# A lag of three chunks beside the attention, a staging tile that outlives it, and new due times: sparse attention followed by two feed-forward layers on one Trainium2 core

## The chip, the cores and the metric

The kernel runs on one core of one Trainium2 chip, as one program. The metric is the device time of the program in microseconds. Timed runs are separate executions; the profile is one further execution, taken by the hardware profiler. The engines are TensorE (PE, with its weight loads as PEld), VectorE (DVE), ScalarE (ACT), GpSimd (POOL) and SyncE (SP), which only issues DMAs.

## The reference

```python
# q, k, v: (4, 8, 576, 64), tau: a number
scores = scale * np.matmul(q, k.transpose(0, 1, 3, 2))          # scale = 1/8
thresh = np.max(scores, axis=-1, keepdims=True) - tau
scores = np.where(scores >= thresh, scores, -1000000000.0)
attn = softmax(scores)                                          # in words here
x = (attn @ v) laid out as (2304 tokens, 512)
h = x @ w1_in                                                   # (2304, 2048)
g = np.where(h > 0.0, h, np.exp(np.minimum(h, 0.0)) - 1.0)
x = g @ w1_out                                                  # (2304, 512)
h = x @ w2_in
out = np.maximum(0.01 * h, h) @ w2_out
```

## The kernel before, in words

**Attention.** The 32 heads are taken in pairs, and the 576 rows of queries of a batch in two groups, of 4 and of 5 units of 64 rows (`GROUPS`). So there are 4 batches x 2 groups x 4 pairs = 32 groups. Two units at a time go through this line: TensorE makes the scores s into two PSUM banks (L475), VectorE scales them and takes the maximum (L479) and the threshold (L485), ScalarE cuts (L490) and exponentiates (L493), VectorE inverts the sum (L496), GpSimd multiplies by it (L498). The result e then has to be turned. For the first four groups TensorE turns it (L513) and ScalarE or VectorE copies it to p (`copies`, by `kc`). For the other 28 VectorE turns it in blocks of 32 (L518) and 16 DMAs per group bring the blocks to their places (L568): `NG` of the 16 are issued by GpSimd, the others by SyncE. Then TensorE makes v, the product of p and the values (L582), and a copy puts it into x.

**Feed-forward.** The hidden width of 2048 is cut into 16 chunks of 128. A chunk of h needs 12 products (4 chunks of x times 3 products of rounded parts, since each fp32 operand is split into a high part, xh, gh, wih, woh, and a low part, xl, gl, wil, wol); a chunk's share of y needs 12 too. Between them stand the steps of g: exponential (L639, ScalarE), minus one (L641 on VectorE or L643 on GpSimd, by `km`), maximum with h (L647, VectorE), rounding to gh (L313 ScalarE, L311 GpSimd, by `kg`) and the subtraction that gives gl (L307 VectorE, L308 GpSimd). While the attention runs, the first 7 blocks of 256 tokens go through the first 8 chunks of layer 0 ("beside the attention"); the very first of them uses plain fp32 products (L621, L674). After it, the remaining 512 tokens go through the same 8 chunks, then all 2304 tokens through the other 8 and then through layer 1, in blocks of 512.

**Lag and buffers.** In `block`, the products of y for chunk j are made after those of h for chunk j + `LAG`; `moe_rings` gives gh and gl `LAG + 1` buffers. h has two halves of one PSUM bank. The sums of y of a block are copied to the tile ysa (`evac_a`), and that is written to DRAM (L731, yp).

**Order.** No engine's order is written by hand. Every step becomes an `Op` with dependencies, a due time `vt` and a list of engines with costs. `Order.run` goes through time and on each free engine starts the ready step that is due first; the instructions are emitted in that order, and on the chip the engines wait for each other by semaphores. All due times come from the table `KN`: `boff`, `bdt`, `yoff` and `mo` place the blocks beside the attention, the time per chunk, the products of y and the steps of g; `o1` to `o6` the steps of the attention; `wv0`, `wv1`, `wp0` the weights; `vl` the loads of the values. On TensorE, `stay` lets a step of the same kind as the last one (plain fp32, or rounded) go first if it is due no more than that many ns after the first in line.

**The end of the attention.** `end_a` is a step of the planner that closes the pools of the attention and opens those of the rest over the same memory. It waits for every step that has been listed up to it.

Of the kernel before, what the change touches and what calls it, by code (L numbers as in the profile page):

```python
# [10 lines left out]
F32 = mybir.dt.float32  # L11
F32R = mybir.dt.float32r
# [9 lines left out]
NP = NH // 2  # L22
# [7 lines left out]
NU = S // 64  # L30
GROUPS = [(b, u0, u1) for b in range(B) for u0, u1 in ((0, 4), (4, NU))]
UM = 5
WT = 32 * UM
BESIDE = 7
GP = 1
PT = ()
NG = 5
POOLI = 520
SPI = 720
PM = ()  # L40
# [4 lines left out]
SX = 640  # L45
LAG = 2
TAUX = 100.0
LN9 = -20.72326583694641
# [3 lines left out]
KN = dict(  # L52
    pad=18, stay=1957.74, late=1.3, margin=0, look=0.00236881, warm=2, tu=2525.65, lead=19496.6, wv0=975.379,
    wv1=-2861.01, early=3673.33, boff=26347.2, bdt=5788.03, yoff=6965.78, coff=5895.83, wb=140.292, w2a=-207.297,
    b0=0, b1=0, b2=0, bd0=9322.68, vl=22862.5, tl=13509.4, wp0=137202, wp1=-2346.6, o1=-5700.07, o2=1859.51,
    o3=-792.8, o4=-3200.93, o5=4767.88, o6=-24.0285, mo=-2162.59, ka='P', kl='PA', kh='PA', ko='P', kt='D', kx='A',
    kxl='DP', km='DP', kg='A', kgl='DP', kgl1='D', kd='P', kc='AD', kn='P', kv='AD')

# [204 lines left out]
def attn_moe_kernel(ctx, tc, kqv, tau, w1i, w1o, w2i, w2o, yp, out):  # L263
# [19 lines left out]
    wa_r = ring(stg, 1, [128, 512], F32, "wa_")  # L283
    ysx = []
    ys_r = Ring(lambda: ysx[-1], 1)
# [77 lines left out]
    def moe_rings(pool, w):  # L363
        xr = [[ring(pool, 1, [128, w], F32R, f"x{z}{k}") for z in "hl"] for k in range(KC)]
        return xr, ring(pool, 2, [128, w], F32, "g"), *(ring(pool, LAG + 1, [128, w], F32R, n) for n in ("gh", "gl"))

# [12 lines left out]
    rings = {True: moe_rings(sbuf(aes, "ma"), TA)}  # L379
    ysx.append(ac.tile([128, KC, TA], F32, name="ysa"))  # L380
    taut = ac.tile([128, 1], F32, name="taut")
# [45 lines left out]
    def group(gi, p, vts, held=None):  # L427
# [23 lines left out]

        by_pe = gi < GP or p in PT
        which = len(p_r.gens) % 2
# [10 lines left out]
        def units(js, vt):  # L464
# [4 lines left out]
            def qk():  # L469
                for z, j in enumerate(js):  # L470
                    for h in range(2):
                        for i in range(2):
# [11 lines left out]
                             out=thr()[:, 0:m], in0=nm()[:, 0:m], scalar1=taup, scalar2=1.0, op0=ALU.add, op1=ALU.mult)),  # L484
                         D=(150, lambda: nc.vector.tensor_scalar(  # L485
                             out=thr()[:, 0:m], in0=nm()[:, 0:m], scalar1=taup, scalar2=None, op0=ALU.add))),
# [201 lines left out]

    ypdone = {}

    def block(layer, t0, fs, tb, deps, hps, yrings, evac, vt0, dt, reg=False):
        if reg and t0 < NATIVE * TA:
            xc = [(None, x[:, k, t0:t0 + tb], deps[k]) for k in range(KC)]
        else:
            xc = conv_x(t0, tb, deps, vt0 - dt + (KN["coff"] if reg else 0), reg)
        pend, lasty = [], None
        if isinstance(yrings, Ring):
            gen = yrings.new()
            ybank = [(gen, m % 2, m % 2 == 1) for m in range(KC)]

            def ysl(yg, m):
                return yg()[:, m // 2, m % 2 * TA:(m % 2 + 1) * TA]
        else:
            ybank = [(r.new(), 0, True) for r in yrings]

            def ysl(yg, m):
                return yg()[:, 0:tb]
        for n in range(len(fs) + LAG):
            if n < len(fs):
                pend.append(step_h(layer, fs[n], tb, xc, hps, vt0 + n * dt, reg))  # L710
            if n >= LAG:
                j = n - LAG
                lasty = step_y(layer, fs[j], j == 0, j == len(fs) - 1, tb, pend[j], ybank, ysl,
                               vt0 + n * dt + (KN["yoff"] if reg else 1))
        evac(t0, tb, ybank, ysl, lasty, xc, vt0 + len(fs) * dt)

    def evac_a(t0, tb, ybank, ysl, last, xc, vt):
        ys = ys_r.new()
        done = []
        if ybank[0][0] is ybank[1][0]:  # L720
            yg = ybank[0][0]
            for j in range(2):
                done.append(op(copy_of("AD", 2 * TA, lambda j=j: ys()[:, 2 * j:2 * j + 2, 0:TA],
                                       lambda j=j: yg()[:, j, :].rearrange("p (a b) -> p a b", a=2)),
                               [last[2 * j], last[2 * j + 1]], [yg, ys], vt))
# [33 lines left out]
    for b in range(B):  # L759
        mine = [gi for gi, g in enumerate(GROUPS) if g[0] == b]  # L760
        order += [(gi, p) for p in range(NE) for gi in mine] if b in PM else [(gi, p) for gi in mine for p in range(NE)]
    kept, ready = None, {}
    for gi, p in order:
        b, u0, u1 = GROUPS[gi]
# [5 lines left out]
        held = later  # L770
        if gi < GP or p in PT or u == NP * NU:
            held()
            held = None
# [14 lines left out]

    for i in range(BESIDE):
        need = next(n for t, n in ends if t >= (i + 1) * TA)  # L790
        block(0, i * TA, list(range(FH)), TA, x_deps(i * TA, TA), h_a, ya, evac_a,
              need * TU + KN["boff"] + (KN["b0"], KN["b1"], KN["b2"], 0)[min(i, 3)], KN["bd0"] if i == 0 else KN["bdt"],
              reg=True)
        if i == NATIVE - 1:
# [3 lines left out]

    end_a = op((HOST, 0, lambda: close_attn()), list(od.ops), [], 0)
    late_pool = []  # L800
# [14 lines left out]

    rest = [(t0, tb) for t0, tb in ((t, min(TB, NT - t)) for t in range(BESIDE * TA, NT, TB))]
    ysb = {}
# [75 lines left out]
```

## Time and profile before

| | us |
|---|---|
| three timed runs | 1047.26, 1040.55, 1043.79 |
| their median | 1043.79 |
| the profiled execution | 1044.41 |
| its span from first to last instruction | 1042.6 |
| mean granted clock of TensorE | 0.992 of full speed |

The 0.6 us by which the profiled execution lies above the median are less than the runs differ among themselves. The span leaves out 1.8 us around the program. In the rows below, times are in us from the start of the span unless marked ns, and L475 is line 475 of the kernel. Ends of matmuls are modelled, so rows of TensorE overlap; the distance of two starts is the better measure of what a product takes.

### The profile page before, as it was taken

How to read it: one execution, taken by the hardware profiler on the slowest of the kernel's cores; microseconds unless marked ns; L12 is line 12 of the kernel's file. 1: busy time of each engine (PE TensorE's matmuls, PEld its weight loads, DVE VectorE, ACT ScalarE, POOL GpSimd, SP SyncE). 2: the span in 40 equal slices, each digit the busy share in tenths (PEclk: the TensorE clock that was granted, in tenths of full speed). 3: DMA queues.
4: the chain of work that ended last, by engine and by line, in shares of the span. 5: the costliest groups of instructions: out<-in, count | busy, mean ns of one | idle time of the engine just before them, and what ended most of it. 6: DMA issues, size and time to landing. Idle time of an engine off the chain costs nothing.

```text
span 1042.6 us, 17014 instructions
## 1 busy us (share of the span) xinstructions
PE 1005.2 (96%) x6228; PEld 795.3 (76%) x6228; DVE 569.2 (55%) x1146; ACT 507.0 (49%) x1009; POOL 392.0 (38%) x542
## 2 busy tenths in 40 slices
PE   6869999999999998999999999999999999999998
PEld 3446676677676776888888889888888888888898
DVE  6888778787887856767786457442211311311121
ACT  6967767677777753555455235432222311322221
POOL 5678977567577752444443013440000000000000
PEclk8999999999999999999999999999999999999999
DMA  6676876766778653353443103320100100000010
GB/s 213 209 216 175 221 195 192 227 188 196 201 209 240 192 150 119 102 182 101 143 141 101 61 21 86 118 61 0 41 1 1 41 1 1 22 19 1 1 41 21
DMA packets 47554, 115.93 MB, mean 111 GB/s; under 512 B 9776, under 2 KB 14384, under 8 KB 47472
## 3 DMA queue, kind: packets, MB, share of 16 engines
q1 hardware_dynamic: 42960, 104.36, 33.4%
q0 software_dynamic: 4512, 10.50, 3.7%
q8 instruction: 49, 0.80, 0.3%
q14 instruction: 33, 0.27, 0.1%
HBM read 67.63 MB, written 9.44 MB: 74 GB/s over the span
## 4 chain that ended last, share of the span: by engine, by line
PE 90%; DVE 3%; DMA 2%; ACT 2%; issue 1%; POOL 0%; SPq 0%; ACTq 0%; DVEq 0%; POOLq 0%
PE y L678 37%; PE h L624 22%; PE hb L624 15%; PE v L582 7%; PE s L475 7%; PE y L674 1%; DMA p<-t 1%; PE h L621 1%; DVE w L346 1%; DMA taut<-in_tau_dram 1%; DVE ss L479 1%; DMA wraw<-in_w1i_dram 1%; PE y L513 0%; DVE xl L307 0%; ACT e L493 0%
## 5 line engine op out<-in xcount | busy, mean ns | idle before, releaser
L307 DVE TENSOR_TENSOR gl<-g,gh 128x512 fp32r<-128x512 f32 (+1 forms) x150 | 101.1, 675 | 284.4 <-ACT g L656 265.0
L678 PE MATMUL y<-gh,woh 128*128 128x512 f32 (+1 forms) x704 | 245.5, 349 | 2.1 <-ACT ysa L318 1.4
L678 PE MATMUL y<-gl,woh 128*128 128x512 f32 (+1 forms) x704 | 242.8, 345 | 0.0
L624 PE MATMUL h<-xh,wih 128*128 128x256 f32 (+1 forms) x448 | 153.1, 342 | 9.2 <-ACT g L639 5.1
L678 PEld LDWEIGHTS y<-gh,woh 128*128 128x128 f32 x704 | 132.5, 188 | 29.1 <-issue 8.8
L624 PE MATMUL h<-xl,wih 128*128 128x256 f32 (+1 forms) x448 | 148.6, 332 | 0.7 <-DVE xl L307 0.6
L678 PEld LDWEIGHTS y<-gl,woh 128*128 128x128 f32 x704 | 132.7, 188 | 16.1
L498 POOL TENSOR_SCALAR e<-e,su 128x576 f32<-128x576 f32 x144 | 113.9, 801 | 32.2 <-DVE su L496 30.9
L678 PE MATMUL y<-gh,w 128*128 128x256 f32 (+1 forms) x384 | 124.9, 325 | 0.0
L490 ACT ACTIVATE ss<-ss,thr 128x576 f32<-128x576 f32 x144 | 104.6, 767 | 34.5 <-DVE thr L485 34.4
L479 DVE TENSOR_SCALAR_CACHE_REDUCE ss<-s,scl 128x576 f32<-128x576 f32 x144 | 113.8, 798 | 10.9 <-PE s L475 10.7
L678 PE MATMUL y<-gh,wol 128*128 128x512 f32 (+1 forms) x320 | 117.7, 368 | 0.0
L518 DVE STREAM_TRANSPOSE t<-e 128x640 f32<-128x640 f32 x128 | 101.2, 823 | 17.9 <-POOL e L498 12.5
L493 ACT ACTIVATE e<-ss,taun 128x577 f32<-128x577 f32 x144 | 110.5, 768 | 0.3
L624 PEld LDWEIGHTS h<-xh,wih 128*128 128x128 f32 x448 | 84.2, 188 | 33.2 <-issue 8.8
L475 PE MATMUL s<-in 64*64 64x288 f32 x1152 | 91.3, 428 | 7.8 <-DVE ss L479 7.8
L624 PE MATMUL hb<-xh,wih 128*128 128x512 f32 (+1 forms) x256 | 94.6, 369 | 0.0
L624 PE MATMUL hb<-xl,wih 128*128 128x512 f32 (+1 forms) x256 | 94.5, 369 | 0.0
L582 PE MATMUL v<-p,v 128*64 128x320 f32 (+1 forms) x640 | 87.1, 417 | 5.3 <-DVE p L319 2.3
L624 PEld LDWEIGHTS h<-xl,wih 128*128 128x128 f32 x448 | 84.3, 188 | 10.0 <-DVE xl L307 1.8
L624 PE MATMUL h<-xh,w 128*128 128x256 f32 (+1 forms) x288 | 89.3, 310 | 0.0
L654 ACT ACTIVATE gh<-h 128x512 fp32r<-128x512 f32 (+1 forms) x40 | 22.2, 555 | 132.4 <-PE h L624 132.4
(207 smaller groups left out, 1591.4 us busy)
## 6 DMA issues: line engine op xcount, KB each, us to landing
p<-t SPq DMA_DIRECT2D x128, 100.0 KB, 2.8
p<-t SPq DMA_DIRECT2D x144, 80.0 KB, 3.3
v<-in_kqv_dram SPq DMA_DIRECT2D x32, 320.0 KB, 3.8
in<-in_kqv_dram SPq DMA_DIRECT2D x16, 608.0 KB, 4.2
in<-in_kqv_dram SPq DMA_DIRECT2D x16, 544.0 KB, 4.0
wraw<-in_w1i_dram SPq DMA_DIRECT2D x16, 512.0 KB, 4.3
wraw<-in_w1o_dram SPq DMA_DIRECT2D x16, 512.0 KB, 3.6
wraw<-in_w2i_dram SPq DMA_DIRECT2D x16, 512.0 KB, 3.5
```

The lines of the kernel that those rows point to most:

```text
L307: return pick(who, D=(dve(n), lambda: nc.vector.tensor_tensor(**args()), PORT), P=(pool_tt(n), lambda: nc.gpsimd.tensor_tensor(**args())))
L346: ob = op((DVE, dve(512), lambda: nc.vector.scalar_tensor_tensor(out=b().bitcast(U32), in0=top(), scalar=0x80000000, in1=b().bitcast(U32), ...
L475: nc.tensor.matmul(s[z]()[64 * h:64 * h + 64, i, 0:HALF], q()[r, at:at + 64], k()[r, h], start=True, stop=True)
L479: om = [op((DVE, dve(S) + 160, lambda z=z: nc.vector.tensor_scalar(out=ss[z]()[:, 0:S].rearrange("p (j c) -> p j c", j=2), in0=s[z]()[:, : ...
L490: o = op((ACT, act(S) + 95, lambda z=z: nc.scalar.activation(out=ss[z]()[:, 0:S], in_=ss[z]()[:, 0:S], func=AF.Prelu, bias=thr()[:, z:z + ...
L493: oe.append(op((ACT, act(S) + 190, lambda z=z: nc.scalar.activation(out=e[z]()[:, 0:S + 1], in_=ss[z]()[:, 0:S + 1], func=AF.Exp, bias=tau ...
L498: on = [op(pick(KN["kn"], P=(pool_ts(S) + 90, lambda z=z: nc.gpsimd.tensor_scalar(out=e[z]()[:, 0:S], in0=e[z]()[:, 0:S], scalar1=su()[:, ...
L518: turned.append(op((DVE, dve(SX) + 70, lambda z=z, cols=cols: nc.vector.transpose(out=blocks(tg).rearrange("p d c q -> p c d q")[:, :, :, ...
L582: nc.tensor.matmul(ps()[64 * h:64 * h + 64, 0:64 * n], v()[:, h, c, :], blocks(pg)[:, 2 * h:2 * h + 2, c], start=(c == 0), stop=(c == 4))
L624: nc.tensor.matmul(hp(), w_()[:, cs], x_()[:, 0:tb], start=(k == 0 and z == 0), stop=(k == KC - 1 and z == 2))
L654: o1 = op((ACT, actp(tb), lambda: nc.scalar.activation(out=gh()[:, cs], in_=hp(), func=AF.Prelu, alpha=0.01)), [o], [hg, gh], vt)
L678: nc.tensor.matmul(ysl(yg, m), w_()[:, cs], g_()[:, 0:tb], start=(first and z == 0 and share == 0), stop=(last and z == 2 and end))
```

## The change

- Beside the attention the lag of y behind h is three chunks (`LAGB`) instead of two, and gh and gl have four buffers of 256 columns instead of three. After the attention the lag stays two.
- The staging tile ysa is allocated in the pool `const`, which stays open to the end, and no longer in `ac`, which closes with the attention. `end_a` waits for the steps that were listed up to the last block's `evac_a`, not for that block's copies and its write.
- `NG` goes from 5 to 4: GpSimd issues 4 of the 16 turning DMAs of a group, SyncE 12. The cost of such an issue in the planner goes from 720 to 700.
- `kc`: the copies of the first four groups go to ScalarE alone. `km`: minus one goes to GpSimd alone, in all of layer 0. `kg`: the rounding of g beside the attention goes from ScalarE to GpSimd. `ko`: the low part of late weights may go to VectorE also.
- Most due times of `KN` change, `stay` from 1958 to 7715 among them.
- New names (`HEADS`, `FIRST`, `CUTS`, `LP`) write the same blocks, the same groups and an empty list `PT` in another way.

```diff
+CUTS = (4,)
-GROUPS = [(b, u0, u1) for b in range(B) for u0, u1 in ((0, 4), (4, NU))]
+GROUPS = [(b, u0, u1) for b in range(B) for u0, u1 in zip((0, *(CUTS if b == 0 else (4,))), (*(CUTS if b == 0 else (4,)), NU))]
+HEADS = [(0, 256)]
+FIRST = HEADS + [(t, TA) for t in range(256, 1792, TA)]
-BESIDE = 7
-PT = ()
-NG = 5
+PT = set()
+NG = 4
+LP = 0
-SPI = 720
+SPI = 700
 LAG = 2
+LAGB = 3
 KN = dict(
-    pad=18, stay=1957.74, late=1.3, margin=0, look=0.00236881, warm=2, tu=2525.65, lead=19496.6, wv0=975.379,
-    wv1=-2861.01, early=3673.33, boff=26347.2, bdt=5788.03, yoff=6965.78, coff=5895.83, wb=140.292, w2a=-207.297,
-    b0=0, b1=0, b2=0, bd0=9322.68, vl=22862.5, tl=13509.4, wp0=137202, wp1=-2346.6, o1=-5700.07, o2=1859.51,
-    o3=-792.8, o4=-3200.93, o5=4767.88, o6=-24.0285, mo=-2162.59, ka='P', kl='PA', kh='PA', ko='P', kt='D', kx='A',
-    kxl='DP', km='DP', kg='A', kgl='DP', kgl1='D', kd='P', kc='AD', kn='P', kv='AD')
+    pad=18, stay=7714.83, late=1.3, margin=0, look=0.00215667, warm=2, tu=2531.97, lead=19496.6, wv0=-3582.57,
+    wv1=-2667.23, early=3947.77, boff=35320.1, bdt=7245.69, yoff=9100.82, coff=9376.59, wb=-808.91, w2a=-228.739,
+    b0=0, b1=0, b2=0, bd0=9449.23, vl=44286.3, tl=27712.7, wp0=148302, wp1=-2346.6, o1=-9300.97, o2=-137.82,
+    o3=-3325.49, o4=-608.895, o5=2620.38, o6=-24.2237, mo=-15328.7, ka='P', kl='PA', kh='PA', ko='PD', kt='D',
+    kx='A', kxl='DP', km='P', kg='P', kgl='DP', kgl1='D', kd='P', kc='A', kn='P', kv='AD')
...
-    ysx = []
+    ysx = [const.tile([128, KC, TA], F32, name="ysa")]
...
-        return xr, ring(pool, 2, [128, w], F32, "g"), *(ring(pool, LAG + 1, [128, w], F32R, n) for n in ("gh", "gl"))
+        return xr, ring(pool, 2, [128, w], F32, "g"), *(ring(pool, (LAGB if w == TA else LAG) + 1, [128, w], F32R, n) for n in ("gh", "gl"))
...
-    ysx.append(ac.tile([128, KC, TA], F32, name="ysa"))
...
+    since = [0]
+
-    def block(layer, t0, fs, tb, deps, hps, yrings, evac, vt0, dt, reg=False):
-        if reg and t0 < NATIVE * TA:
+    def block(layer, t0, fs, tb, deps, hps, yrings, evac, vt0, dt, reg=False, whole=False):
+        if whole:
...
-        for n in range(len(fs) + LAG):
+        lag = LAGB if reg else LAG
+        for n in range(len(fs) + lag):
             if n < len(fs):
                 pend.append(step_h(layer, fs[n], tb, xc, hps, vt0 + n * dt, reg))
-            if n >= LAG:
-                j = n - LAG
+            if n >= lag:
+                j = n - lag
...
     def evac_a(t0, tb, ybank, ysl, last, xc, vt):
+        since[0] = len(od.ops)
         ys = ys_r.new()
...
-    end_a = op((HOST, 0, lambda: close_attn()), list(od.ops), [], 0)
+    end_a = op((HOST, 0, lambda: close_attn()), od.ops[:since[0]], [], 0)
```

## Rows read from the trace of the kernel before

**Rows 1.** Part 1 of the page: busy us, share of the span, instructions.

```profile
PE 1005.2 (96%) x6228; PEld 795.3 (76%) x6228; DVE 569.2 (55%) x1146; ACT 507.0 (49%) x1009; POOL 392.0 (38%) x542
```

**Rows 2.** Windows: length, then busy us (instructions) of each engine, clock, DMA.

```profile
core 0: us, PE busy (x) PEld busy (x) DVE busy (x) ACT busy (x) POOL busy (x), PEclk, DMA share, GB/s
50.00:75.00 25.00, 17.64 (x124) 10.29 (x116) 22.88 (x47) 19.55 (x40) 17.82 (x25) 0.93 0.74 221
...
300.00:325.00 25.00, 24.47 (x228) 17.52 (x228) 19.89 (x52) 19.68 (x44) 19.10 (x32) 1.00 0.78 219
...
450.00:475.00 25.00, 25.00 (x112) 20.71 (x111) 16.75 (x26) 12.84 (x21) 8.23 (x9) 1.00 0.54 184
```

**Rows 3.** Timeline of TensorE, 64 to 95 us: start, duration, and idle time before.

```profile
64.79 0.72 PE L475 MATMUL s<-in 64*64 64x288 f32 x8 [2.41 <-DVE ss L479]
...
76.56 4.93 PE L582 MATMUL v<-p,v 128*64 128x320 f32 x20 [2.20 <-DMA p<-t]
...
92.10 2.91 PE L582 MATMUL v<-p,v 128*64 128x320 f32 x20
```

**Rows 4.** Waits of TensorE, 100 to 405 us: total us, times, longest.

```profile
PE h L624 <- ACT g L639: 5.1, 10, 0.5
...
PE h L624 <- DVE g L647: 1.7, 3, 0.6
PE y L678 <- ACT ysa L318: 1.4, 2, 0.7
```

**Rows 5.** Timeline of TensorE around one batch of s, 145 us.

```profile
145.01 0.28 PE L624 MATMUL h<-xl,wih 128*128 128x256 f32 x1
145.13 0.28 PE L624 MATMUL h<-xh,w 128*128 128x256 f32 x1
145.34 1.20 PE L475 MATMUL s<-in 64*64 64x288 f32 x16
146.47 0.39 PE L624 MATMUL h<-xh,wih 128*128 128x256 f32 x1
146.69 0.28 PE L624 MATMUL h<-xl,wih 128*128 128x256 f32 x1
```

**Rows 6.** The chain of waits at the boundary, 380 to 410 us: start, us, what.

```profile
385.12 2.84 PE v L582 x20
...
395.20 0.70 DVE ysa L319
...
397.32 3.58 DMA yp_dram<-ysa
...
401.39 0.64 ACT xh L313
...
402.80 1.65 PE h L624 x6
...
405.90 2.75 PE hb L624 x12
```

**Rows 7.** Timelines of TensorE and VectorE at the boundary: the last v, its copy.

```profile
396.50 3.12 PE L582 MATMUL v<-p,v 128*64 128x320 f32 x20
...
399.66 0.49 DVE L319 COPY x<-v 128x320 f32<-128x320 f32 x1 [2.36 <-PE v L582]
```

**Rows 8.** Groups by line and form: count, busy us, mean ns, idle before.

```profile
L568 POOL DMA_DIRECT2D p<-t x140 | 70.5, 508 | 23.1 <-DVE t L518 9.5 <-PE s L475 5.4 <-DVE ss L479 3.0
...
L313 ACT ACTIVATE gh<-g 128x256 fp32r<-128x256 f32 x56 | 23.0, 411 | 22.5 <-DVE g L647 15.4 <-PE y L678 6.9
...
L643 POOL TENSOR_SCALAR g<-g 128x256 f32<-128x256 f32 x41 | 17.0, 415 | 17.8 <-ACT g L639 17.5
...
L641 DVE TENSOR_SCALAR g<-g 128x256 f32<-128x256 f32 x23 | 7.7, 343 | 5.0 <-ACT g L639 4.8
...
L319 DVE COPY p<-y 128x640 f32<-128x640 f32 x5 | 4.1, 813 | 0.3 <-PE y L513 0.3
```

**Rows 9.** The same view: minus one on 512 columns, after the attention.

```profile
L641 DVE TENSOR_SCALAR g<-g 128x512 f32<-128x512 f32 x37 | 23.2, 628 | 35.8 <-ACT g L639 35.5
```

**Rows 10.** Timeline of SyncE, 173 us: the issues of one group.

```profile
173.26 6.92 SPq L568 DMA_DIRECT2D p<-t  x11
```

More of the change, by code (lines that the diff above doesn't have):

```diff
@@ L450, in q @@
             return kq()[:, at0:at0 + 128 * n]
-        by_pe = gi < GP or p in PT
+        by_pe = gi < GP or (gi, p) in PT
         which = len(p_r.gens) % 2
@@ L484, in units @@
                              out=thr()[:, 0:m], in0=nm()[:, 0:m], scalar1=taup, scalar2=1.0, op0=ALU.add, op1=ALU.mult)),
-                         D=(150, lambda: nc.vector.tensor_scalar(
+                         A=(200, lambda: nc.scalar.activation(
+                             out=thr()[:, 0:m], in_=nm()[:, 0:m], func=AF.Identity, bias=taup)),
+                         D=(270, lambda: nc.vector.tensor_scalar(
                              out=thr()[:, 0:m], in0=nm()[:, 0:m], scalar1=taup, scalar2=None, op0=ALU.add))),
@@ L701, in ysl @@
             def ysl(yg, m):
-                return yg()[:, m // 2, m % 2 * TA:(m % 2 + 1) * TA]
+                return yg()[:, m // 2, m % 2 * TA:m % 2 * TA + tb]
         else:
@@ L722, in evac_a @@
             for j in range(2):
-                done.append(op(copy_of("AD", 2 * TA, lambda j=j: ys()[:, 2 * j:2 * j + 2, 0:TA],
-                                       lambda j=j: yg()[:, j, :].rearrange("p (a b) -> p a b", a=2)),
+                done.append(op(copy_of("AD", 2 * tb, lambda j=j: ys()[:, 2 * j:2 * j + 2, 0:tb],
+                                       lambda j=j: yg()[:, j, :].rearrange("p (a b) -> p a b", a=2)[:, :, 0:tb]),
                                [last[2 * j], last[2 * j + 1]], [yg, ys], vt))
@@ L762, in attn_moe_kernel @@
     kept, ready = None, {}
+    PT.update(order[len(order) - LP:])
     for gi, p in order:
@@ L770, in attn_moe_kernel @@
         held = later
-        if gi < GP or p in PT or u == NP * NU:
+        if gi < GP or (gi, p) in PT or u == NP * NU:
             held()
@@ L787, in x_deps @@
                  if b * S + 64 * u0 < t0 + tb and b * S + 64 * u1 > t0] for k in range(KC)]
[L789 to L793, printed above, removed]
+    for i, (t0, tb) in enumerate(FIRST):
+        need = next(n for t, n in ends if t >= t0 + tb)
+        block(0, t0, list(range(FH)), tb, x_deps(t0, tb), h_a, ya, evac_a,
+              need * TU + KN["boff"] + (KN["b0"], KN["b1"], KN["b2"], 0)[min(i, 3)],
+              KN["bd0"] if i < NATIVE else KN["bdt"], reg=True, whole=i < NATIVE)
         if i == NATIVE - 1:
@@ L814, in dt @@
         return 24 * mm(tb)
-    rest = [(t0, tb) for t0, tb in ((t, min(TB, NT - t)) for t in range(BESIDE * TA, NT, TB))]
+    rest = [(t0, tb) for t0, tb in ((t, min(TB, NT - t)) for t in range(sum(FIRST[-1]), NT, TB))]
     ysb = {}
```

## The prediction

> **What bounds the kernel now.** I read part 1 of the page first: TensorE is counted busy for 96% of the span [rows 1]. That says which engine to follow, not where time can still be won, so the second view is the table of windows [rows 2]. Three kinds of stretch are to be seen in it. From 450 to 475 us, after the attention, TensorE is busy for 25.00 us of 25: there the matmuls follow each other without a hole and nothing in this diff removes one of them. From 300 to 325 us, beside the attention, TensorE has 24.47 of 25 while VectorE has 19.89, ScalarE 19.68 and GpSimd 19.10, so no other engine is full. From 50 to 75 us TensorE has only 17.64 while VectorE has 22.88, and the granted clock is 0.93. So the change can win something only before about 406 us, and I looked for the TensorE time that is lost there, in three places.
>
> The start. TensorE waits 2.41 us for VectorE's reading of s and 2.20 us for the turned p, and the 20 products of v behind that last wait take 4.93 us, where the same 20 take 2.91 us fifteen us later [rows 3]. The waits are followed by a lower clock, so a hole costs more than its length.
>
> Beside the attention (111 to 395 us). TensorE waits visibly for the parts of g, 5.1 us in 10 waits on ScalarE's exponential and 1.7 us on VectorE's maximum, and 1.4 us on the copy to y's staging tile [rows 4]. Besides, it pays for every change between plain fp32 products (s, v) and rounded ones (h, y). A steady run of h spaces its products by 0.12 us (145.01 and 145.13). In [rows 5] the s batch starts 0.21 us after the last h product, 0.09 more than the spacing, and the second h product starts 0.22 us after the first, 0.10 more. That is 0.19 us for each excursion. I counted 53 excursions between 111.4 and 394.9 us: 10.1 us in all.
>
> The boundary between the attention and the rest. The chain of waits [rows 6] goes from the copy of y to its staging tile (395.20 us), over the write of that tile to DRAM (3.58 us from 397.32), to the first xh (401.39), the first products of h, slowly (402.80), and full speed at 405.90. The last plain products were issued by 395.0 us. Of the 10.9 us from there to 405.90, TensorE has use for 0.36 (three products of y at 0.12), 2.84 (the last v [rows 7], at the pace of the v in the chain) and 2.75 (one chunk of h, 12 products of 512 columns): 5.0 us are lost.
>
> **The change part by part.** The sum of matmuls, of elements and of bytes is the same: seven blocks of 256 tokens stand beside the attention before and after, the groups are cut the same, and the list of turns by TensorE is empty in both. What changes is order, buffers and who does what.
>
> *The staging tile.* It moves out of the pools that close after the attention, and the close no longer waits for the last block's copies and its write. What is late next is the last v (396.50 + 2.84, so near 399.34 us) and its copy to x, 0.49 us from 399.66 [rows 7]; only the fourth chunk of x needs that copy. If the order stays, the first xh moves from 401.39 to about 399.34: 2.05 us won. If v is placed ahead of the last y, what stays is the way from the first xh to the first h, 402.80 - 401.39 = 1.4 us [rows 6]: 5.0 - 1.4 = 3.6 us won. A smaller gain would need another transfer into that memory, and I see none; none at all is the floor. I take **2.7 us**, nearer to the first end, since the order was not written for this.
>
> *The planner's stay, from 1958 to 7715.* TensorE's order keeps to one kind of product while its best candidate is due within that time of the other kind. That should make the 53 excursions fewer. In the stretch there are 58 batches of s and 24 of v; two s batches can't follow each other, because both s banks are in VectorE's hands, so the longest excursion is s, v, s and at least 58 - 24 = 34 are left. The most that can be won is 19 x 0.19 = 3.6 us; if longer runs of h and y make s late, it could be a loss of about 1 us, one wait such as the 2.41 us one spread over fewer places. I take half of the most, **1.9 us**.
>
> *Lag three, four buffers of gh and gl, g's chain ahead of the softmax (its offset from -2162 to -15329), blocks due 9 us later.* This gives TensorE up to 36 products of y (12 a chunk, 4.3 us at 0.12) that wait for nobody, where there were 24, and gives ScalarE and VectorE g's steps earlier. It is aimed at the 6.8 us of [rows 4]. The lag itself does not free h's bank, which is what h waits for; the priority does. Bounds: 0 and the 8.2 us of the three rows. I take **3.0 us**.
>
> *Group 0's copies of p, ScalarE alone instead of either.* Five copies of 813 ns leave VectorE [rows 8], 4.1 us, where VectorE is the fullest engine (22.88 of 25) and ScalarE has 19.55. They lie in the first 57 us. With weights due 4.6 us earlier and s read 3.6 us earlier in the due times, the start is a reshuffle whose size the trace cannot show. Bounds: the hole of [rows 3] closes (2.41 + 2.20 of waits and 4.93 - 2.91 = 2.0 of clock: 6.6 us) or one more such hole opens (-4). I take **2.0 us**, the half of VectorE's relief.
>
> *GpSimd gets g - 1 always and the rounding of g.* On 256 columns 23 subtractions leave VectorE (343 ns) and cost 415 on GpSimd; 48 roundings beside the attention leave ScalarE, at 411 ns each, and cost GpSimd the same 415, its one-input form [rows 8]. That is 23 x 0.415 + 48 x 0.415 = 29.5 us more on GpSimd. One transfer less in 16 for the 28 groups that turn by DMA takes 28 x 0.508 = 14.2 us off it [rows 8]. Net +15 us over some 330: 19.1 of 25 becomes 20.2. GpSimd is off the chain, so I cost it at nothing; the cover is the room in these 25, and the waiting e tiles behind the new work are the fourth rival. On 512 columns, after the attention, 37 subtractions of 628 ns move too [rows 9]; at the ratio above, 415 / 343, they take some 760 ns on GpSimd, in a stretch where TensorE has no hole, a chunk of h and y lasts 2 x 2.75 us and GpSimd has 8.23 of 25: nothing.
>
> The Trainium skill, GPSIMD Engine Reference, "4.1 Engine selection", speaks against such a move: elementwise work belongs on VectorE, GpSimd being about twice as slow for two-input operations. The same table calls one-input work roughly line rate, and the rows agree with that half: 415 against 343 ns. Were the factor two to hold here, the 71 steps would cost 71 x 0.27 = 19 us more on GpSimd, an estimate from that page, and still sit beside TensorE.
>
> *The 28 transfers that go to SyncE.* SyncE issues 11 a group in 6.92 us [rows 10], 0.63 each, so each group's turned p is complete 0.63 us later, and behind the twelfth stand the loads of v and of the next group and the write of y. v's load is also due 21 us later. A group lasts about 284 / 24 = 11.8 us and its twelve transfers take 7.6: SyncE has room for the rest. If the cover (36 products of y) is gone, v waits: 24 x 0.63 = 15 us. I cost it at nothing.
>
> **The sum.** 2.7 + 1.9 + 3.0 + 2.0 = 9.6 us. The profiled execution took 1044.4 us (span 1042.6), so 1034.8; it lies 0.6 above the median of the three runs (1043.8), so I predict 1034.2, rounded to **1034 us**.
>
> **The rivals.** *Only the boundary pays* (1041 us, 1038 to 1045). TensorE is at 24.47 of 25, and 6.8 us of waits may simply move from g to the reading of s. For it: no engine beside TensorE is relieved by much. Against it: the excursions are counted, not guessed. *The start and the middle both close* (1022 us, 1014 to 1029): all upper ends, 3.6 + 3.6 + 8.2 + 6.6 = 22 us. For it: almost every due time is new. Against it: upper ends rarely come together. *The change doesn't do what it says*: the lag of three is used up by h's two half banks, the h products still wait for the exponential, and the sum loses the 3.0: 1037 us, inside the forecast's own range. *GpSimd's queue makes the softmax late* (1057 us, 1047 to 1064): the normalising of e stands behind g - 1 and a rounding, 0.82 us, so the turn, the transfers and v come 0.82 us later in each of 24 groups, 19.7 us. The 3.0 of g are lost with it: 1034 + 3 + 19.7 = 1057, and 1047 if half of it shows. It decides as soon as the delay, with the 0.63 us of SyncE, outlasts the products of y that TensorE has in hand. Against it: 4.3 us of them against 1.45.
>
> [...]
>
> **How the numbers follow.** The forecast with its own range (1029 to 1038, the case of the lag without use in it) gets 0.52, only the boundary 0.22, both close 0.18, GpSimd's queue 0.08. A measurement of this kernel tells about 1% from no change, 10.4 us. Faster by more than that is under 1033.4: all of "both close" and half of the forecast, 0.44. Slower by more is over 1054.2: over half of the last, and some for a hole at the start that no rival names, 0.07. The rest, 0.49, is within. The range 1022 to 1045 leaves out the lower half of "both close" and the last rival.
>
> **What would show it.** Right: the write of y's staging tile is gone from the chain at the boundary and the first xh follows the last v by under 0.2 us; excursions between 111 us and the boundary number 40 to 46; h's waits on the exponential are under 4 us; full speed of h starts about 9.6 us earlier than 405.9. Wrong: TensorE's waits for p or for VectorE's reading of s grow beside the attention, GpSimd shows over 21 of 25, or the start shows another hole with the clock under 0.93. The stretch after the boundary should keep its length, 1042.6 - 405.9 = 636.7 us; a change there would be one that I have not seen.

## The result, and the profile after

| | before | after |
|---|---|---|
| median of five timed runs, us | 1042.65 | 1051.52 |
| lowest to highest, us | 1040.55 to 1047.26 | 1050.73 to 1054.21 |
| the profiled execution; its span, us | 1044.41; 1042.6 | 1054.21; 1052.4 |
| start of `hb` (full speed) in the chain of waits after the attention, us | 405.90 | 416.02 |
| span from there to the end, us | 636.7 | 636.4 |

The ratio is 1.0082, interval 1.0054 to 1.0110: 0.8% slower, where 1.0% faster was forecast and 1045 us was the upper end of the range. All of it lies ahead of the boundary, where the gain was expected. (The profiled execution of after is the slowest of its five, so its trace shows some 2.7 us more than the median.)

Part 1 of the page of after: busy us, share of the span, instructions.

```profile
PE 1010.7 (96%) x6228; PEld 795.5 (76%) x6228; DVE 575.0 (55%) x1129; ACT 491.1 (47%) x961; POOL 372.6 (35%) x579
```

Against [rows 1], TensorE's share is the same and GpSimd is counted busy for 19 us less. So the page's first part doesn't tell what became slower. The windows of after, with the columns of [rows 2]:

```profile
core 0: us, PE busy (x) PEld busy (x) DVE busy (x) ACT busy (x) POOL busy (x), PEclk, DMA share, GB/s
50.00:75.00 25.00, 19.10 (x133) 10.86 (x126) 21.28 (x47) 21.76 (x43) 15.84 (x24) 0.86 0.80 213
125.00:150.00 25.00, 21.53 (x200) 15.51 (x192) 17.98 (x46) 14.62 (x34) 21.30 (x34) 1.00 0.74 200
300.00:325.00 25.00, 24.53 (x229) 18.12 (x228) 18.85 (x48) 18.00 (x40) 18.55 (x32) 1.00 0.75 222
```

From 300 to 325 us TensorE does what it did. From 125 to 150 us it runs 200 matmuls; the same window of before has 222:

```profile
125.00:150.00 25.00, 23.99 (x222) 17.78 (x214) 18.84 (x49) 18.71 (x43) 19.54 (x32) 1.00 0.79 217
```

To follow a loss through an order that is new everywhere, I took the time from the span's start and subtracted what the matmuls issued by then take at their steady spacing (0.07 us for s, 0.14 for a turn and for a v of 320 columns, 0.12 for a v of 256, 0.117 for 256 columns of h or y, 0.227 for 512, and 0.216 for the plain products of the first block). What remains is TensorE time lost, by my own count, in one execution of each kernel; the last column is the trace's:

| lost, us | to 100 | 100 to 150 | 150 to 375 | 375 to 425 | full speed of `hb` at |
|---|---|---|---|---|---|
| before | 35.8 | 4.5 | 19.3 | 6.2 | 405.90 |
| after | 35.8 | 9.0 | 23.8 | 7.2 | 416.02 |

In these two traces the start is as long as it was, 4.5 us more are lost round the passage from the first block to the second, 4.5 in small pieces beside the attention, and the last stretch, 375 to 425 us, loses 1.0 more instead of winning. How much of each difference is that of the execution, and not of the order, change 18 shows below. TensorE's waits of after, 100 to 415 us, in the form of [rows 4]:

```profile
PE h L629 <- ACT g L644: 5.4, 11, 0.5
PE h L629 <- DVE g L652: 2.5, 5, 0.6
PE s L478 <- DMA in<-in_kqv_dram: 2.4, 3, 1.2
```

The waits that lag and priority were aimed at are no shorter (5.1 and 1.7 before). New is s waiting for its own load. The loads come late in SyncE's timeline of after:

```profile
118.33 10.15 SPq L573 DMA_DIRECT2D p<-t  x12
128.58 0.53 SPq L439 DMA_DIRECT2D in<-in_kqv_dram  x1
...
130.39 10.23 SPq L573 DMA_DIRECT2D p<-t  x12
140.72 0.53 SPq L439 DMA_DIRECT2D in<-in_kqv_dram  x1
...
141.83 8.84 SPq L573 DMA_DIRECT2D p<-t  x12
```

Twelve transfers take 8.8 to 10.2 us here, not the 7.6 of the prediction, and the loads come behind them. (The prediction read its price, 6.92 us for eleven, at 173 us; in this stretch the eleven of before take 6.8 to 9.9.) In another execution of the same order, change 18 below, s doesn't wait for its load at all, so this wait belongs to the one execution. The chain of waits at the boundary of after:

```profile
406.82 2.66 PE y L683 x21
409.50 0.70 DVE ysa L323
410.25 0.63 PE y L683 x3
410.95 0.64 ACT xh L317
411.66 1.29 POOL xl L312
412.99 3.02 PE h L629 x11
416.02 2.73 PE hb L629 x12
```

Against [rows 6] the write to DRAM is gone. The last v is now ahead of the last two chunks of y, and xh waits for those. Of the 9.2 us from 406.82 to 416.02, 2.8 are y and 2.7 a chunk of h: 3.7 lost, against 5.0. So the boundary itself wins 1.3 us, and what the last column but one of the table loses lies on either side of it.

### The profile page after: what moved, and what is told of

Read it like the earlier page. It is cut to its first block, busy times and chain, and to the rows that moved or that the text cites. A ratio compares the mean times of both kernels' runs of the same rounds, so it can differ in the third digit from the quotient of the medians.

```text
span 1052.4 us, 17049 instructions
## 1 busy us (share of the span) xinstructions
PE 1010.7 (96%) x6228; PEld 795.5 (76%) x6228; DVE 575.0 (55%) x1129; ACT 491.1 (47%) x961; POOL 372.6 (35%) x579
## 4 chain that ended last, share of the span: by engine, by line
PE 85%; DMA 4%; ACT 3%; SPq 2%; DVE 2%; issue 2%; POOL 2%; DVEq 0%; ACTq 0%; POOLq 0%
PE y L683 35%; PE h L629 21%; PE hb L629 15%; PE v L587 6%; PE s L478 5%; SPq L573 2%; DMA in<-in_kqv_dram 2%; DMA p<-t 1%; PE y L679 1%; ACT e L498 1%; ACT ss L495 1%; PE h L626 1%; DMA v<-in_kqv_dram 1%; DMA taut<-in_tau_dram 1%; POOL e L503 1%
## 5 line engine op out<-in xcount | busy, mean ns | idle before, releaser
L648 POOL TENSOR_SCALAR g<-g 128x256 f32<-128x256 f32 (+1 forms) x104 | 55.1, 530 | 157.6 <-ACT g L644 155.2
L478 PE MATMUL s<-in 64*64 64x288 f32 x1152 | 93.7, 436 | 9.1 <-DVE ss L482 6.4
```

The lines of the kernel that those rows point to most:

```text
L478: nc.tensor.matmul(s[z]()[64 * h:64 * h + 64, i, 0:HALF], q()[r, at:at + 64], k()[r, h], start=True, stop=True)
L648: P=(pool_ts(tb), lambda: nc.gpsimd.tensor_scalar(out=g()[:, cs], in0=g()[:, cs], scalar1=-1.0, scalar2=1.0, op0=ALU.add, op1=ALU.mult))),
```

## The experiments

Theory one (L in the expectations): the lag and the buffers themselves cost, at the passages between blocks. Theory two (G, P and S): the engines' new work and SyncE's queue cost. Theory three (T and D; R): the due times cost, or every change of them reshuffles the order by as much. Ratios are to the kernel before, run on the same chip in turns with the experiment (its medians there 1043.7 to 1044.9). The runs were made in five groups on three chips, so kernels are compared by these ratios, and a difference of them is turned into us with 1044.5.

### The structure alone

Change 1, `e1_struct_oldtab`: the staging tile, the early close, the lag and the buffers of after, with everything else of before.

```diff
-NG = 4
+NG = 5
-SPI = 700
+SPI = 720
-KN = dict(... the table after ...)
+KN = dict(... the table before ...)
-                         D=(270, lambda: nc.vector.tensor_scalar(
+                         D=(150, lambda: nc.vector.tensor_scalar(
```

The last two lines are the planner's price of the threshold, a part of the change that its description leaves out. Change 2, `e2_ysa_only`, goes on from there with the lag of before, so that the staging tile and the close are left. Change 3, `e3_lag_only`, is change 1 with the close of before. Change 4, `e4_before_tu`, is the kernel before with one due time moved by 0.05%, which asks nothing but what a reshuffle of the order costs.

```diff
# e2_ysa_only
-LAGB = 3
+LAGB = 2
# e3_lag_only
-    end_a = op((HOST, 0, lambda: close_attn()), od.ops[:since[0]], [], 0)
+    end_a = op((HOST, 0, lambda: close_attn()), list(od.ops), [], 0)
# e4_before_tu
-tu=2525.65
+tu=2527.0
```

> The new structure (lag of three, four buffers, staging tile that outlives the attention, close without the last copies) under the old table: old due times, old engines, 5 turning transfers a group on GpSimd. Theory S (the loss comes from SyncE, where 12 transfers a group stand before the loads of the next group): no loss here, the boundary's 1 to 3 us won, 1040 us against 1043, no wait of s for its load. Theory L (the lag itself makes TensorE's order worse): 1048 to 1052. Theory R (any reshuffle of the planner moves the time by this much): anything from 1036 to 1052.

> Old table, lag of two and three buffers; only the staging tile outlives the attention and the close doesn't wait for the last copies. All theories: the stretch beside the attention keeps its order, and only the boundary moves: first full-speed product of h 1.3 to 3.6 us earlier than 405.9, 1040 to 1042 us against 1043.

> Old table, lag of three and four buffers, the staging tile in the open pool, but the close still waits in the planner for the last copies and their write. Theory S and theory G (the loss comes from the steps of g that went to GpSimd): within 2 us of before, 1041 to 1045. Theory L: 1047 to 1052. Theory R: anything from 1036 to 1052.

> The kernel before with one due time changed by 0.05% (the time per unit, 2525.65 to 2527.0): nothing that any theory prices, so its distance from before is what a reshuffle of the planner alone is worth. Theory R: 3 us or more either way. Theories S, G and L: under 2 us.

| | median us | ratio (interval) | `hb` at |
|---|---|---|---|
| e1_struct_oldtab | 1047.37 | 1.0035 (1.0016 to 1.0053) | 409.29 |
| e2_ysa_only | 1041.73 | 0.9974 (0.9960 to 0.9988) | 403.33 |
| e3_lag_only | 1048.79 | 1.0045 (1.0028 to 1.0063) | 410.49 |
| e4_before_tu | 1046.76 | 1.0021 (1.0003 to 1.0039) | 410.15 |

The staging tile wins 2.7 us and the lag of three costs 6.4 on top of it by the ratios, 5.6 by the medians. In e2_ysa_only every engine carries out the steps of before in the same order up to 402 us; change 1 differs from it by lag and buffers alone. Chain of waits at the boundary of e2_ysa_only:

```profile
395.89 3.06 PE v L587 x20
...
399.77 0.70 DVE xl L311
400.51 2.82 PE h L629 x11
403.33 2.72 PE hb L629 x12
```

The write is gone, and the first xh, at 398.98 us, waits for the last v alone, as the prediction had it. From the last v to full speed it is 7.44 us (395.89 to 403.33), where it was 9.40 (396.50 to 405.90): 1.96 won. The other 0.6 us at `hb` are there before the last v, where the order is the same. The timeline of TensorE in e3_lag_only, where the second block begins:

```profile
123.96 0.39 PE L629 MATMUL h<-xh,wih 128*128 128x256 f32 x1 [1.67 <-ACT xh L317]
125.65 0.55 PE L629 MATMUL h<-xl,wih 128*128 128x256 f32 x1 [1.30 <-POOL xl L312]
...
128.33 0.41 PE L629 MATMUL h<-xh,wih 128*128 128x256 f32 x1
128.55 0.41 PE L629 MATMUL h<-xl,wih 128*128 128x256 f32 x1
```

and the chain of waits of the same run there:

```profile
112.55 3.67 PE y L679 x16
116.24 0.69 DVE ysa L323
...
118.97 1.75 POOL p L573 x4
...
122.75 1.46 POOL e L503 x2
...
124.87 0.73 POOL xl L312
125.65 1.42 PE h L629 x5
```

After the last h of the first block the lag leaves 32 plain products of y, 24 before; the last 16 run in one piece here, and copies, turning, GpSimd's issues and normalising stand between them and the next block's xl. TensorE waits 1.67 + 1.30 us, and then its products come 0.21 us apart instead of 0.12. The count puts 10.1 us of loss between 100 and 150 us (4.5 before, 6.9 in e2_ysa_only with the order of before) and 22.0 from 150 to 375 (19.3 in both). So about half of the lag's cost lies at this passage; the rest, beside the attention, is not traced to waits. Change 3 loses only 4.0 us between 375 and 425 us, although its close still waits in the planner for the write: the tile's place alone takes the write off the chain, and up to the boundary its order is that of change 1. Change 4 sets a measure for what follows: +2.2 us, interval 0.3 to 4.1, for a change that means nothing. TensorE's order there differs from before only from 359 us on. Differences of that size between two orders tell nothing of their cause.

### Taking one part of after back

Change 5, `e5_after_ng5`: SyncE issues 11 again. Change 6, `e6_after_oldletters`: the four engine choices of before. Change 7, `e7_after_vl`: the loads of v due as before. Change 8, `e8_after_lag2`: the lag of before.

```diff
# e5_after_ng5
-NG = 4
+NG = 5
# e6_after_oldletters
-ko='PD', km='P', kg='P', kc='A'
+ko='P', km='DP', kg='A', kc='AD'
# e7_after_vl
-vl=44286.3
+vl=22862.5
# e8_after_lag2
-LAGB = 3
+LAGB = 2
```

> The changed kernel with 5 turning transfers a group on GpSimd and 11 on SyncE, as before. Theory S (twelve issues a group fill SyncE, and the loads of the next group come late): the waits of s for its load, 3.7 us lost behind v in the trace of the changed kernel, fall under 1 us and the time by 2 to 4 us, to 1048. Theory T (the new due times put the load behind the turning transfers whatever their number): 1050 to 1053, the waits stay. Theory R (a reshuffle alone): 2 us either way without the waits going.

> The changed kernel with the old choice of engines: minus one on VectorE or GpSimd, rounding of g on ScalarE, group 0's copies on either, low parts of late weights on GpSimd. Theory G (g's steps on GpSimd hold h's bank longer): the waits of h on g's exponential and maximum, 7.9 us, fall to 5 and the time by 3 us or more, to 1048. Theories S and T: no change beyond 2 us, 1050 to 1053.

> The changed kernel with the old due time of v's loads (22.9 us after the first due time of the group's load instead of 44.3). Theory T as far as it is v's load: SyncE's order goes back to v's load apart from the group's load, waits of s for its load fall under 2 us, 1049. Theory S: no change, 1050 to 1053.

> The changed kernel with the lag of two and three buffers. Theory L (the lag of three costs what it cost under the old table, 4.3 us, most of it in the hole where the second block's first chunk waits for its xh and xl): 1047, and the loss from 111 us to the boundary falls by 3 us or more. If the new due times were made for the lag of three: 1052 or more.

| | median us | ratio (interval) |
|---|---|---|
| e5_after_ng5 | 1053.99 | 1.0087 (1.0058 to 1.0116) |
| e6_after_oldletters | 1063.82 | 1.0181 (1.0149 to 1.0213) |
| e7_after_vl | 1050.57 | 1.0062 (1.0043 to 1.0081) |
| e8_after_lag2 | 1053.48 | 1.0088 (1.0060 to 1.0116) |

No part taken back brings the time back. In changes 5 and 7 the waits of s for its load are gone, and the time against after's ratio of 1.0082 is +0.5 and -2.1 us, with intervals that overlap after's. Since they are gone in change 18 too, with after's order, their going can't be put to these changes; in any case they are not what the change loses. The lag, which cost 6.4 us in the old order, gives nothing back when it is taken out of the new one (+0.6). The old engine choices cost 10.3 us under the new due times.

### Due times by groups

Change 9, `e9_oldtimes`: every number of `KN` as before, the letters, `NG` and `SPI` as after. Changes 10 to 12 take a group of due times back.

```diff
# e9_oldtimes: all numbers of KN as before
# e10_blocks
-boff=35320.1, bdt=7245.69, yoff=9100.82, coff=9376.59, bd0=9449.23
+boff=26347.2, bdt=5788.03, yoff=6965.78, coff=5895.83, bd0=9322.68
# e11_softmax
-vl=44286.3, o1=-9300.97, o2=-137.82, o3=-3325.49, o4=-608.895, o5=2620.38, o6=-24.2237
+vl=22862.5, o1=-5700.07, o2=1859.51, o3=-792.8, o4=-3200.93, o5=4767.88, o6=-24.0285
# e12_gorder
-mo=-15328.7
+mo=-2162.59
```

> The changed kernel (lag of three, staging tile, new engines, 12 transfers on SyncE) with every due time, stay and look of before. Theory D (the new due times are what costs beyond the lag; engines and SyncE's twelfth transfer are hidden): 1047 to 1048, as the run of the new structure under the whole old table. Theory S: 1051 and waits of s for its load or of v for its turned p. If the new engines need the new times: 1055 or more.

> The changed kernel with the old due times of the blocks beside the attention alone (start, time per chunk, offset of y, offset of xh and xl, first block's time per chunk). Theory D as far as it is the blocks' lateness: TensorE gets h and y earlier, less of them is left for the stretch after the last s, 1047. If the softmax's due times are at fault: 1050 to 1054.

> The changed kernel with the old due times of the attention's steps (six offsets, and v's load). Theory D as far as it is these: the waits of s for its load go and the loss before 111 us falls by 2, 1047. If the blocks' times are at fault: 1050 to 1054.

> The changed kernel with the old due time of g's steps (2.2 us ahead of their chunk of h instead of 15.3). My prediction's step (g's priority frees h's bank and is worth 3.0 us): 1054 or more, the waits of h on exponential and maximum grow from 7.9 to over 10 us. If the priority is worth nothing: 1050 to 1053. If it makes the softmax late: 1048.

| | median us | ratio (interval) | lost to 100 | 100 to 150 | 150 to 375 |
|---|---|---|---|---|---|
| e9_oldtimes | 1052.89 | 1.0080 (1.0064 to 1.0095) | 43.1 | 4.7 | 21.3 |
| e10_blocks | 1069.88 | 1.0245 (1.0225 to 1.0265) | 38.5 | 6.0 | 34.2 |
| e11_softmax | 1056.89 | 1.0120 (1.0105 to 1.0135) | 44.2 | 6.6 | 20.9 |
| e12_gorder | 1049.25 | 1.0049 (1.0032 to 1.0066) | 36.9 | 7.6 | 21.1 |

With the old times the new engines lose 7.3 us more at the start than after does. The place is TensorE's timeline in e9_oldtimes:

```profile
88.00 3.57 PE L478 MATMUL s<-in 64*64 64x288 f32 x24 [4.21 <-DVE ss L482]
```

and the chain of waits there runs over GpSimd:

```profile
80.07 2.38 POOL e L503 x3
...
83.17 0.40 POOL g L648
83.57 1.24 POOL w L312
...
87.16 1.47 POOL p L573 x3
...
89.47 1.48 POOL e L503 x2
...
93.18 3.78 PE h L626 x8
```

Minus one (L648), low parts of weights and issues stand in one line with the normalising; the granted clock of 75 to 100 us is 0.80. After's times don't have this hole and lose more later (9.0 for 4.7 between 100 and 150 us, 23.8 for 21.3 up to 375, in these executions), so the new times together cost 0.2 us, nothing by the intervals. Taking back only the block times (+17.0) or only the softmax times with vl (+4.0) is worse than taking all: the price of a group depends on the others. The earlier g, priced as a part of 3.0 us won, has cost 3.4 if anything; the intervals overlap.

### One part of the engine choices on the best structure

Changes 13 to 16 add one part each to e2_ysa_only.

```diff
# e13_tile_ng4
-NG = 5
+NG = 4
# e14_tile_minus1
-km='DP'
+km='P'
# e15_tile_round
-kg='A'
+kg='P'
# e16_tile_copies
-kc='AD'
+kc='A'
```

> The kernel with only the staging tile moved (1041.7 us), and 4 turning transfers of a group on GpSimd, 12 on SyncE. Theory S: 2 to 4 us slower, with waits of v for its turned p or of s for its load. Theory P (GpSimd is the engine that opens the hole at the start, so work taken from it can only help): 1040 to 1042.

> Only the staging tile moved, and minus one on GpSimd alone. Theory P: the first block's eight minus-one steps stand in GpSimd's queue behind weights and e; a hole between 75 and 100 us with s waiting for VectorE or h for g, the clock under 0.9 there, 1045 to 1049. My prediction's step (hidden): 1041 to 1043.

> Only the staging tile moved, and the rounding of g beside the attention on GpSimd instead of ScalarE. The first block has no such rounding, so theory P gives no hole before 111 us; 48 steps of 0.415 us more on GpSimd from 111 us on. Hidden: 1041 to 1043. If GpSimd's queue makes the softmax late there too: 1046 or more.

> Only the staging tile moved, and the first four groups' copies of p on ScalarE alone. My prediction's step (VectorE is the fullest engine up to 75 us and loses 4.1 us of work): 1 to 3 us faster, 1039 to 1041. If ScalarE becomes the one that the turning waits for: 1043 to 1045, with more waits of the turns for ScalarE's copies than the 5.0 us of before.

| | median us | ratio (interval) | against e2, us | `hb` at | after it |
|---|---|---|---|---|---|
| e13_tile_ng4 | 1048.97 | 1.0042 (1.0026 to 1.0057) | +7.1 | 407.52 | 636.7 |
| e14_tile_minus1 | 1051.20 | 1.0059 (1.0038 to 1.0079) | +8.9 | 407.49 | 641.3 |
| e15_tile_round | 1040.20 | 0.9961 (0.9943 to 0.9980) | -1.4 | 401.17 | 636.2 |
| e16_tile_copies | 1050.84 | 1.0050 (1.0032 to 1.0068) | +7.9 | 411.28 | 636.3 |

(The profiled execution of e13_tile_ng4 was the fastest of its ten, 1046.02, so its trace shows less than the median.) The kernel with minus one on GpSimd loses in two places. The hole at the start that theory P expected isn't one of them: the clock of 75 to 100 us is 1.00. By the count 4.1 us more than in e2_ysa_only are lost from 150 to 375 us. The other place is after the boundary, where the prediction priced it at nothing; TensorE in e14_tile_minus1:

```profile
486.09 0.51 PE L683 MATMUL y<-gh,woh 128*128 128x512 f32 x1 [2.14 <-ACT gh L317]
```

GpSimd's timeline in the same run:

```profile
481.76 1.29 POOL L312 TENSOR_TENSOR wol<-w,woh 128x512 fp32r<-128x512 f32 x1 [2.44 <-ACT woh L317]
483.01 0.65 POOL L334 TENSOR_SCALAR wa__5711<-wraw 128x512 f32<-128x512 f32 x1
483.63 0.61 POOL L648 TENSOR_SCALAR g<-g 128x512 f32<-128x512 f32 x1
```

The exponential ended near 483.2; the minus one that it feeds started at 483.63, behind two steps of weights, and ScalarE and VectorE had taken other work meanwhile, so gh came at 485.41 and y at 486.09. From 475 to 500 us GpSimd is busy for 12.72 us of 25. But the queue is not all of it: only six products of y stand there between the block's last h (479.71 us) and the y that needs its gh, where e2_ysa_only and after have 24. From 483.2 the three steps of 0.61, 0.67 and 0.63 us alone would end at 485.1, while TensorE's next product was due at 483.8, so some 1.3 us of the hole, an estimate from these rows, would be there without any queue. In after, where all 40 of these steps are GpSimd's as well, TensorE waits for nothing behind the boundary and the stretch takes 636.4 us.

In e16_tile_copies TensorE's waits from 0 to 111 us hold

```profile
PE h L626 <- DVE gh L652: 5.4, 1, 5.4
PE y L518 <- ACT p L322: 5.2, 7, 1.3
PE v L587 <- ACT p L322: 4.8, 4, 1.8
```

where e2_ysa_only has 0.8 us of the last of these, 4.8 of the second and none of the first, and the clock of 75 to 100 us is 0.90 against 1.00. The last row is no loss by itself: 2.3 us of waits for p from VectorE and 2.2 for p from a transfer are gone for it. The loss is the first row, and it goes over GpSimd, whose timeline there shows

```profile
71.16 0.64 POOL L334 TENSOR_SCALAR wa__780<-wraw 128x512 f32<-128x512 f32 x1 [2.35 <-DMA wraw<-in_w1o_dram]
```

Minus one follows at 72.50 and VectorE's gh at 75.11, both behind the steps of that late weight. How ScalarE's copies, which end before 57 us, lead there is not shown. The rounding alone is not slower; its 1.4 us are within what a reshuffle does, so I call it no cost, not a gain. e15_tile_round has the lowest median of the study and beats both before and after; its interval overlaps that of e2_ysa_only.

### Two due times together, and a change that leaves the order as it was

```diff
# e17_gorder_vl
-vl=44286.3, mo=-15328.7
+vl=22862.5, mo=-2162.59
# e18_after_tu
-tu=2531.97
+tu=2530.5
```

> The changed kernel with the old due times of g's steps and of v's load, the two that alone gave 1049.3 and 1050.6 against 1051.5. If the two losses are causes of their own: 1048, and the loss from 125 to 400 us under 28 us. If each run is only another reshuffle: 1047 to 1055, and no sum.

> The changed kernel with the time per unit changed by 0.06% (2531.97 to 2530.5), which no theory prices. A reshuffle's worth: within 2 us of 1051.5 if the holes belong to the table, up to 5 us off if they belong to the exact order.

e17_gorder_vl took 1050.73 us (1.0068, 1.0048 to 1.0087), e18_after_tu 1053.15 (1.0080, 1.0053 to 1.0107). The two steps that alone gave -2.1 and -3.4 us give -1.5 together, less than either.

Change 18 is not the second reshuffle that it was meant to be. In its trace every engine carries out the same list of steps in the same order as in after (6228 matmuls, 1129 steps on VectorE, 579 on GpSimd, 497 issues on SyncE). So it is after once more, -0.2 us by the ratios, and it shows how far two executions of one order differ. By the count of lost time:

| lost, us | order | to 100 | 100 to 150 | 150 to 375 | 375 to 425 |
|---|---|---|---|---|---|
| before | of before | 35.8 | 4.5 | 19.3 | 6.2 |
| e2_ysa_only | of before to 402 us | 32.8 | 6.9 | 19.3 | 4.1 |
| after | of after | 35.8 | 9.0 | 23.8 | 7.2 |
| e18_after_tu | of after | 36.5 | 7.7 | 21.5 | 9.6 |

Up to 375 us a column of one order moves by up to 3.0 us from one execution to the next. After loses more than before from 100 to 375 us in both of its executions (32.8 and 29.2 against 23.8 and 26.2), but how much in which stretch can't be read from one trace each. And single due times of the size of changes 7, 12 and 17 can't be told from reshuffles.

## Why the prediction was wrong, step by step

The ratios make one path from before to after with a measured step at each place: 0.9974 with the staging tile (-2.7 us), 1.0035 with lag and buffers (+6.4), 1.0080 with the new engines, `NG` and the planner's two prices (+4.7), 1.0082 with the new due times (+0.2): +8.6 in all. On another path the steps have other sizes: the engine choices cost 4.7 with `NG` under the old times, and win 10.3 under the new ones.

*The staging tile, 2.7: right* by e2_ysa_only, in mechanism and nearly in size: the write is off the chain and the last v is what is late. From the last v to full speed 1.96 us are won, near the 2.05 of the first end. That the ratio gives 2.7 (interval 1.3 to 4.2) to the digit is luck. (The products that the prediction has issued by 395.0 us are the rounded ones of y, not plain ones; the sum of 5.0 stands.) In after itself the boundary wins 1.3 (5.0 lost before, 3.7 now): v stands ahead of y there, the case priced at 3.6, but two chunks of y are behind v, xh waits for them, and the first xl is GpSimd's, 1.29 us.

*The planner's stay, 1.9: no gain seen.* After has 51 excursions between 111 and 395 us; 53 were before and 40 to 46 expected. The planner may stay longer, but s is due when it is due: an argument, since the stay was not tried alone. The price of an excursion holds: the 26 in before that are one batch of 16 s each lose 0.21 us. Its reason doesn't follow: from 112.17 to 112.84 us of before, two plain products of y stand between rounded ones of h and the 0.67 us are their steady spacings, nothing lost. s and v differ from h in shape also (weights of 64 by 64 and 128 by 64 against 128 by 128).

*Lag, buffers and g's priority, 3.0: the step that failed first.* The lag costs 6.4 us on the old table, and the waits of [rows 4] stay as they were with the priority as well (5.4 and 2.5 us in after for 5.1 and 1.7). I priced it by waits that it might remove and gave 0 as the lower bound. The prediction itself said that the lag doesn't free h's bank; it should have followed the leftover products to a block's end, where 32 products of y instead of 24 keep the next block's first steps back: TensorE then waits 1.67 and 1.30 us for xh and xl. Taken out of after, the lag gives nothing back, so its 6.4 us are those of the old table.

*Group 0's copies, 2.0: wrong sign alone*, +7.9. VectorE was relieved of 4.1 us, but the same waits for p came back under ScalarE's name, and a hole of 5.4 us opened at 70 us, with the clock down behind it. The lower bound of -4 was such a hole, named without its place; why it opens is not shown.

*Minus one at nothing: wrong alone*, +8.9; in the traces 4.2 before the boundary and 5.0 after it. For the steps behind the boundary it was right in after itself, 636.4 us for 636.7. The busy share of GpSimd was the wrong cover: what counts is what is ahead of a step in its queue when its input comes, and how many products TensorE has left to do meanwhile. The rounding at nothing was right. The Trainium skill, GPSIMD Engine Reference, "4.1 Engine selection", calls one-input work roughly line rate, and after's 420 ns for minus one and 423 for the rounding against before's 343 on VectorE agree roughly; so it was not the length of the steps. The groups of after:

```profile
L648 POOL TENSOR_SCALAR g<-g 128x256 f32<-128x256 f32 x64 | 26.8, 420 | 41.6 <-ACT g L644 41.1
L315 POOL TENSOR_SCALAR gh<-g 128x256 fp32r<-128x256 f32 x48 | 20.3, 423 | 16.2 <-PE y L683 10.5 <-DVE g L652 4.0 <-DVE su L501 0.6
```

*SyncE's 28 transfers at nothing: half right.* Waits behind them are there in one execution of after's order, 2.4 us, and not in the other, and going back doesn't help after; on e2_ysa_only they cost 7.1 us, for which its trace shows no single wait. Neither waits of v for the turned p nor of s for its load stand among TensorE's from 100 to 410 us there.

*The rivals.* GpSimd's queue has the right sign and its range holds 1051.5, but by luck: v waits for the turned p 0.5 us in all between 100 and 415 us of after, not 0.82 in each group. GpSimd's queue made a hole at the start of change 9, not beside the attention, where the rival had it. *The signs.* Of those named for being wrong, after shows 21.30 us of GpSimd from 125 to 150 us and a clock of 0.86 from 50 to 75; of those for being right, only that the write is gone from the chain. *The range* had the start's unknown at +4 us and no term for reshuffling an order of 17,000 instructions, which alone moved the kernel before by 2.2 us.

**Open.** What in after's order loses the time between 100 and 375 us. No due time can be named for what is lost between 150 and 375: changes 7, 12 and 17 lose 20.6, 21.1 and 21.5 there for 23.8, and so does change 18, 21.5, with after's own order. Where the 7.1 us of change 13 are lost: 2.9 of the 4.2 us in its trace lie between 150 and 375 us, in small pieces. Why after does without the holes that its parts open on e2_ysa_only is argued from change 9 (its times were set for its engines), not shown wait by wait.

## What to carry to other kernels

Where a planner makes the order, the price of a part holds only for the order in which it was read: change one part at a time from the fastest kernel, and run a change that means nothing first, to know how large a difference must be. See in the traces whether it changed the order at all; where it didn't, it tells how far one execution differs from the next, and a stretch of a single trace can't be read more finely than that. A step that moves to a half-idle engine is priced by the queue ahead of it when its input arrives and by the work that its consumer has left, not by the engine's busy share. A longer lag leaves more products over at the end of each block; follow what they keep back.

## What the runs showed of the hardware

After the 1.67 and 1.30 us of waits in e3_lag_only TensorE's granted clock fell. The windows there:

```profile
125.00:130.00 5.00, 3.88 (x18) 3.36 (x22) 3.40 (x9) 2.62 (x6) 5.00 (x7) 0.57 0.75 195
130.00:135.00 5.00, 5.00 (x39) 2.47 (x35) 2.69 (x9) 1.80 (x6) 4.22 (x8) 0.75 0.96 310
```

At 0.57, near the lower of its two levels (1.2 of 2.4 GHz), products of h came 0.21 us apart. The two windows lack 0.43 and 0.25 of 5 us, 3.4 us of full clock, so the hole of 3.0 us cost about twice its length, an estimate from these rows.

VectorE's subtraction for gl on 256 columns took 525 ns in e15_tile_round and 522 in after, where GpSimd does the rounding, and 472 in e2_ysa_only. The Trainium skill, SBUF — State Buffer, "Who interferes with whom", says that a VectorE instruction with two SBUF inputs, as this one, contends with a GpSimd instruction that reads SBUF. The 11% agree in direction, but the rounding is not shown to be their cause: in e13_tile_ng4, where it stays on ScalarE, the subtraction takes 526. The groups of e2_ysa_only and e13_tile_ng4:

```profile
L311 DVE TENSOR_TENSOR gl<-g,gh 128x256 fp32r<-128x256 f32 x46 | 21.6, 472 | 41.9 <-ACT g L661 36.0 <-ACT gh L317 5.7
L311 DVE TENSOR_TENSOR gl<-g,gh 128x256 fp32r<-128x256 f32 x43 | 22.6, 526 | 45.0 <-ACT g L661 36.0 <-ACT gh L317 8.5
```
